# An attention and gated-MLP block on one core: first loads on two queues, and a new written-out order of all jobs

## The chip, the cores and the metric

The kernel runs on one core of a Trainium2 chip. The metric is the device time of one execution in microseconds. A core has TensorE (matmuls, written to PSUM), VectorE (DVE), ScalarE (ACT), GpSimd (POOL) and SyncE (SP), each with an instruction queue of its own that it works off in order; they wait for each other and for DMAs on semaphores.

## The reference

```python
x = A_x                                     # (1, 2048, 448), bfloat16
h = x + attention(layernorm(x))             # 16 heads of 28; token s sees s, s-2, ..., s-14
h2 = h + gmlp(layernorm(h))
# attention: qkv = x @ wqkv; logits = q . k * 28**-0.5 over the 8 offsets; softmax; @ v; @ wo
# gmlp: z = gelu(x @ w_in), w_in 448 x 1792; z1, z2 = the two halves of 896
#   g = w_sp (2048 x 2048) @ layernorm(z2) + b_sp[:, None];   return (z1 * g) @ w_out
```

Both layer norms are without scale and shift. All inputs are bfloat16.

## The kernel before

The 2048 tokens are 16 row tiles of 128 (`x_tm`), the 448 features three chunks of 128 and one of 64. The work is a list of 881 jobs, created in a fixed sequence by loops in the kernel's function and numbered as they are created. Each job belongs to one engine and is one or a few instructions with the resources that it reads and writes. `ORDER` is a list of job numbers, written out as a constant; `Planner.order` returns the jobs in that order, and each engine's queue gets its jobs in it. Semaphore waits follow from the resources alone, so any order that respects them computes the same. Job 880 is a filler: one matmul of 256 columns on a constant tile (`warm`), which keeps TensorE running; it stands in the list as often as wanted. `BANKS` gives each job group that needs PSUM its banks, in a list in the order of creation. `ON` names jobs that run on another engine than their default, `MODE` how the products are split.

The jobs, by their names (m a token tile, b one of 18 attention blocks of some 112 queries and 128 keys, t a group of token tiles, g a group of four heads):

- `x0`, `x1`, `x2`, `x4`, `x6`, `x8`, `x12` load 1, 1, 2, 2, 2, 4 and 4 tiles of x; `wq0` to `wq4` the query and key weights, `wv`, `wv_0`, `wv_1` the value weights, `wo...` the output weights, `w_in...` the MLP's, `bb` the bias b_sp, `w_out`; `wlo`, `whi` load w_sp through a DMA transpose. All DMAs stand on SyncE's queue before.
- `st0_m`, `mv0_m` (VectorE) and `rs0_m` (GpSimd) are the statistics of the first layer norm, `n0_m` (VectorE) normalizes into `xn`; `xT0` to `xT3` transpose on TensorE and `xe0_0`, `xe0_1`, `xe1_0`, `xe2_0`, `xe3_0` move the result to `xhT`; from `xT4` on the transpose is a DMA. `nd0_m`, `nd1_m`, `od_b` are small copies that a DMA transpose needs.
- `wp0` to `wp3` spread wq into padded heads (`wqk`). `qk0F0` to `qk0H` and `qk1...` are the first query-key products, `qk2_g` to `qk5_g` the wider ones, `qe...` their evacuations to `qkT`; `v_b` and `ve_b` the values for two blocks.
- `lg_b_j` (L791) are eight matmuls with 28 rows each, for eight heads' logits, j = 0 on the rows 0 to 63 and j = 1 on the rows 64 to 127; `ex_b_j` (ScalarE) the exponential, `mk_b` (VectorE) the mask, `o_b` (L815) 16 matmuls for the weighted values and the sums, `rc_b`, `om_b` (VectorE) the division into `otm`, `oT_b` a DMA transpose to `OT`, or from block 11 on to `OTs`, from where `oc_b` copies it to `OT`.
- `y_m` is the output projection for two tiles, `h_m` (VectorE) the first residual; `st1`, `mv1`, `rs1`, `n1` its layer norm, `hT_m` the DMA transpose to `hnT`.
- `z2_m` and `z1_u` are the MLP's products, `z2c` a raw evacuation, `z2g`, `z1g` the gelu (ScalarE); `st2`, `mv2`, `rs2`, `n2` the layer norm of z2. `g_i_n` (L964, L985) are the products with w_sp in pieces, `ua`, `um` (VectorE) bias and gate, `wo_m`, `wp12` to `wp15` (L1012, L1033) the last product, `r_m` the second residual, `out_m` the store.

A product of the 448 features (`product`, L459) has two jobs a and b that accumulate in one PSUM tile pair. The last chunk has 64 rows, and two matmuls on 64 rows each can stand in the two halves of the array. `MODE` 'FH' runs six full matmuls and then two half-row ones, 'HF' the other way round; 'AB' cuts the full ones into half-row ones too, 8 in job a and 6 in job b. So TensorE works with 128 rows, 64 rows or 28 rows, and changes between them along its queue.

TensorE's queue before, up to y12b (with x and a number: that many in a row):

```
before: warm x19 xT0 warm x8 qk0F0 qk0F1 qk0F2 qk0H xT1 warm x10 lg0_1 lg0_0 warm qk1F0 xT3 qk1F1 qk1F2 xT2 qk1H v0a
    qk2_3a v0b qk2_3b lg1_0 warm lg1_1 v2a qk2_0a qk2_2a v2b qk2_2b qk2_1a qk2_0b qk2_1b o1 v4a lg3_1 lg2_0 v4b lg2_1
    qk3_1a qk3_0a qk3_3a qk3_0b qk3_2a qk3_3b qk3_2b qk3_1b lg3_0 o0 o2 v6a lg5_1 lg5_0 v6b qk4_3a qk4_2a lg4_0 lg4_1
    qk4_3b qk4_2b qk4_0a lg6_1 qk4_0b qk4_1a lg6_0 o3 o5 lg7_1 qk4_1b y0a lg7_0 o4 lg8_0 o6 lg8_1 y0b v8a v10a lg9_0
    v10b v8b o7 qk5_3a qk5_2a lg9_1 lg11_0 qk5_2b qk5_3b y2a lg11_1 lg10_0 y2b qk5_0a lg10_1 qk5_0b y4a v12a qk5_1a
    y4b o8 qk5_1b lg12_0 v12b lg12_1 o9 lg13_1 o10 v14a lg13_0 v14b lg14_0 lg14_1 o11 o12 z2_1a lg15_1 z2_1b y6a
    lg16_1 lg15_0 y6b lg16_0 o14 o13 lg17_0 lg17_1 z2_0a z2_0b v16a z2_3a y8a v16b z2_2a y8b z2_2b o17 o16 z1_1a z2_4a
    z1_1b z2_3b z2_4b o15 z1_0a y10a z1_0b z2_5a y10b z2_5b z2_6a z1_5a z2_7a z2_6b z1_3a z2_7b y12a z1_3b y12b
```

Of the kernel before, what the change touches and what calls it, by code (L numbers as in the profile page):

```python
# [1111 lines left out]
```

## Time and profile before

| | us |
|---|---|
| median of 3 runs (lowest, highest) | 245.06 (244.08, 245.13) |
| profiled execution | 243.96 |
| its span, first to last instruction | 242.2 |
| TensorE busy | 236.7, 98% |
| VectorE, ScalarE, GpSimd busy | 149.7, 89.8, 37.7 |
| matmuls | 2568, 39 of them fillers |

In the views, PE is the matmul, PEld the weight load, SPq SyncE's queue. A line of the timeline is start, duration, engine, source line, operation, and the wait before it in brackets. A matmul's duration contains its way through the array, so that neighbours overlap; the chain that ended last shows them without overlap. The page's strips show 40 slices of 6.05 us in tenths of busy time. The windows' columns are stretch, its sum, busy time (and instructions) of PE, PEld, DVE, ACT and POOL, the granted clock, the DMA engines' share and GB/s.

### The profile page before, as it was taken

The numbers are of one execution on the slowest core, as the hardware profiler recorded it, in microseconds if no ns is written. First come the engines' busy times: TensorE is split into PE (matmuls) and PEld (weight loads), VectorE is DVE, ScalarE is ACT, GpSimd is POOL, SyncE is SP. The second block draws the span as 40 slices with busy tenths as digits, with TensorE's granted clock in tenths as the row PEclk, the third lists the DMA queues.
The fourth block names the chain that finished last, engine by engine and source line by source line (L and its number), as shares of the span: only waits on it lengthen the run. The fifth ranks groups of instructions, "written<-read, shape, count | busy, mean of one in ns | idle before, by whom it ended". The sixth has DMA issues, their size and how long they took to land.

```text
span 242.2 us, 5928 instructions
## 1 busy us (share of the span) xinstructions
PE 236.7 (98%) x2568; PEld 128.2 (53%) x2568; DVE 149.7 (62%) x336; ACT 89.8 (37%) x107; POOL 37.7 (16%) x90
## 2 busy tenths in 40 slices
PE   6999999999999999999999999999999999999995
PEld 4766545644655454555555555555555555555443
DVE  4799999989999999999800324320610663041834
ACT  4577467775998947959333000000000000000000
POOL 7432312120602023622300100000000000000000
DMA  5955755498477899945989700000100002010202
GB/s 167 293 152 103 117 107 121 138 145 186 97 119 152 165 182 197 194 90 120 164 179 170 152 3 0 0 3 0 41 0 3 1 3 76 0 41 0 78 0 76
DMA packets 66266, 23.21 MB, mean 96 GB/s; under 512 B 58688, under 2 KB 65984, under 8 KB 66240
## 3 DMA queue, kind: packets, MB, share of 16 engines
q1 hardware_dynamic: 66240, 22.83, 45.4%
q8 instruction: 20, 0.33, 0.6%
q14 instruction: 6, 0.05, 0.1%
HBM read 6.72 MB, written 1.84 MB: 35 GB/s over the span
## 4 chain that ended last, share of the span: by engine, by line
PE 80%; DMA 7%; ACT 5%; DVE 5%; SPq 2%; issue 0%; DVEq 0%
PE psum L964 37%; PE psum L459 26%; PE psum L1012 7%; ACT E L800 3%; PE psum L985 3%; DMA hnT<-xn 3%; PE psum L1033 2%; PE psum L791 2%; DMA x_tm<-in_A_x_dram 2%; PE psum L815 2%; DMA OTs<-otm 2%; SPq L517 2%; DVE st L875 1%; ACT V L502 1%; DVE z2p L502 1%; PE psum L692 1%
## 5 line engine op out<-in xcount | busy, mean ns | idle before, releaser
L945 DVE TENSOR_TENSOR ub<-psum,bb 128x512 bf16<-128x512 f32 x28 | 18.1, 685 | 43.1 <-PE psum L964 39.3
L964 PE MATMUL psum<-wsp_hi,z2p 64*128 64x512 bf16 x384 | 43.2, 376 | 0.0
L800 ACT ACTIVATE E<-psum 128x896 bf16<-128x896 f32 (+2 forms) x36 | 31.8, 935 | 8.1 <-PE psum L791 8.1
L964 PEld LDWEIGHTS psum<-wsp_hi,z2p 64*128 64x128 bf16 x384 | 21.7, 94 | 19.4
L875 DVE BATCH_NORM_STATS2 st<-z2p 128x6 f32<-128x448 bf16 x32 | 19.1, 614 | 12.8 <-ACT z2p L871 12.2
L964 PE MATMUL psum<-wsp_lb,z2p 64*128 64x512 bf16 x224 | 26.5, 376 | 0.0
L964 PE MATMUL psum<-wsp_la,z2p 64*128 64x512 bf16 x224 | 26.5, 376 | 0.0
L459 PE MATMUL psum<-w_in,hnT 64*128 64x448 bf16 (+1 forms) x200 | 25.4, 350 | 0.5 <-ACT E L800 0.3
L459 PE MATMUL psum<-hnT,w_in 64*128 64x512 bf16 (+1 forms) x178 | 24.7, 377 | 0.0
L993 DVE TENSOR_TENSOR srg<-psum,x_tm 128x448 bf16<-128x448 f32 (+1 forms) x17 | 9.5, 592 | 23.9 <-PE psum L1012 21.9
L459 PE MATMUL psum<-xhT,wqk 64*128 64x512 bf16 (+2 forms) x218 | 23.8, 349 | 0.2
L608 DVE BATCH_NORM_STATS2 st<-x_tm 128x6 f32<-128x448 bf16 x32 | 18.8, 612 | 2.3 <-DMA x_tm<-in_A_x_dram 2.2
L806 DVE TENSOR_TENSOR E<-E,maskb 128x1792 bf16<-128x1792 bf16 (+2 forms) x18 | 19.6, 1091 | 0.1
L913 ACT ACTIVATE z1p<-psum 128x1024 bf16<-128x1024 f32 x14 | 14.1, 1022 | 13.3 <-PE psum L459 13.1
L964 PEld LDWEIGHTS psum<-wsp_lb,z2p 64*128 64x128 bf16 x224 | 12.7, 94 | 11.4
L964 PEld LDWEIGHTS psum<-wsp_la,z2p 64*128 64x128 bf16 x224 | 12.7, 94 | 11.3
L603 POOL TENSOR_TENSOR rs<-rs,negh 128x2 f32<-128x2 f32 (+2 forms) x23 | 17.6, 764 | 1.9
L1012 PE MATMUL psum<-w_out,z1p 64*128 64x448 bf16 (+1 forms) x154 | 17.4, 349 | 0.0
L459 PEld LDWEIGHTS psum<-w_in,hnT 64*128 64x128 bf16 (+1 forms) x200 | 11.3, 94 | 11.5 <-issue 1.5
L459 PEld LDWEIGHTS psum<-xhT,wqk 64*128 64x128 bf16 (+1 forms) x218 | 10.5, 94 | 9.7 <-ACT E L800 0.5
L459 PEld LDWEIGHTS psum<-hnT,w_in 64*128 64x128 bf16 (+1 forms) x178 | 10.2, 94 | 9.9 <-ACT z2p L868 0.4
L459 PE MATMUL psum<-wv,xhT 64*128 64x448 bf16 (+1 forms) x114 | 14.6, 351 | 0.0
(64 smaller groups left out, 259.3 us busy)
## 6 DMA issues: line engine op xcount, KB each, us to landing
w_in<-in_B_w_in_dram SPq DMA_DIRECT2D x8, 224.0 KB, 3.4
out_dram<-srg SPq DMA_DIRECT2D x16, 112.0 KB, 1.7
x_tm<-in_A_x_dram SPq DMA_DIRECT2D x2, 448.0 KB, 5.8
w_out<-in_B_w_out_dram SPq DMA_DIRECT2D x1, 784.0 KB, 6.6
wq<-in_A_wqkv_dram SPq DMA_DIRECT2D x3, 224.0 KB, 2.8
x_tm<-in_A_x_dram SPq DMA_DIRECT2D x3, 224.0 KB, 4.8
bb<-in_B_b_sp_dram SPq DMA_DIRECT2D x1, 512.0 KB, 5.1
wv<-in_A_wqkv_dram SPq DMA_DIRECT2D x1, 336.0 KB, 5.3
```

The lines of the kernel that those rows point to most:

```text
L459: ins = e.matmul(o, w, x, start=k not in seen, stop=last, **kw)
L603: (lambda e: e.tensor_tensor(R, A, negh[:, 0:1].to_broadcast([128, n]), ALU.pow), [rr, r_negh], r_rs[k][m:m + n])],
L608: [(lambda e: e.bn_stats(st[:, m, :], src), [rsrc], [r_st[k][m]])], dve_t(D))
L800: return e.activation(o, i, AF.Exp, scale=SCALE)
L806: return e.tensor_tensor(a, a, maskb[:, 0:1, pad:pad + nq].to_broadcast([NK, NHEAD, nq]), ALU.mult)
L875: [(lambda e, m=m, k=k: e.bn_stats(st3[:, m, k, :], z2p[:, m, D * k:D * (k + 1)]), [r_z2[m]], [r_st[2][m]])], dve_t(D))
L913: return e.activation(o, i, AF.Gelu_apprx_tanh)
L945: [(lambda e: e.tensor_tensor(ub[:, s, :], psv(tk, k), bb[:, 512 * tc:512 * tc + 512], ALU.add), [r_bb], [r_ub[s]])], dve_t(512), use=[tk] ...
L964: ins = e.matmul(psv(tk, k), z2p[h, s, 128 * fc:128 * fc + 128], wsp(s, tc)[h], start=n == 0 and s == 0, stop=n == len(lots) - 1 and s == ...
L985: ins = e.matmul(psv(tk), z2p[:, s, 128 * fc:128 * fc + 128], wsp(s, tc), start=(s == 0), stop=(s == NB - 1))
L993: [(lambda e: e.tensor_tensor(srg[:, s, c0:c1], psv(tk, k, c1 - c0), x_tm[:, m, c0:c1], ALU.add), [r_x[m]], r_srg[2 * s + (c0 > 0):2 * s + ...
L1012: ins = e.matmul(psv(tk, k, D), z1p[h, fc, 128 * (m + k):128 * (m + k) + 128], w_out[h, fc, :], start=fc == 0 and (which == 0 or not half) ...
```

## The change

The changed kernel has the same jobs and instructions, but for two fillers more (41) and the modes of six products, four of which change the number of matmuls. New values stand for `ORDER`, `BANKS`, `MODE` and `ON`, and `load` lets `ON` choose the queue of a load. `half_t` and two durations have 2.5 ns more per matmul; they served the search and are not used when the order is written out. Of `MODE` six products change: `y8`, `z1_0`, `z1_4` to 'AB', `y10` to 'FH', `z2_0`, `z2_4` from 'HF' to 'FH'.

```diff
@@ load @@
             nload[0] += 1
-            return pl.job(name, eng, nload[0] * 0.001 - 65 if key is None else key,
-                          [(f, list(reads), list(writes), True)], dur, 0.0, after=after, srv=srv)
+            eng = ON.get(name, eng)
+            j = pl.job(name, eng, nload[0] * 0.001 - 65 if key is None else key,
+                       [(f, list(reads), list(writes), True)], dur, 0.0, after=after, srv=srv)
+            if not transpose and not name.startswith("out"):
+                j.alts = {"sp": dur, "act": dur + 0.08}
+            return j
@@ ON @@
+ON = {'x0': 'act', 'wq1': 'act', 'wq2': 'act', 'x1': 'act', 'wv': 'act', 'w_in1_1': 'act', 'w_in2_1': 'act',
+         'w_in3_0': 'act', 'xe1_0': 'dve', ..., 'wp0': 'act', 'wp3': 'act', 'qe3_0': 'dve', ..., 'bb': 'act'}
```

In `ON`, `qe1_1`, `qe2_2` and `qe3_1` are no longer on VectorE, so they fall back to ScalarE; `z2c6` and `z2c13` go to VectorE and `z2c9` back to ScalarE; `oc12` goes to ScalarE, `oc16` and `oc17` to VectorE; `wp0` changes places with `wp2`; and some of the small copies `nd` and `od` change between GpSimd and VectorE.

TensorE's queue after, up to y12b:

```
after: warm x21 xT0 warm x8 qk0F0 qk0F1 qk0F2 qk0H xT1 warm x11 lg0_0 lg0_1 qk1F0 qk1F1 qk1F2 qk1H warm xT3 xT2 v0a
    lg1_0 lg1_1 v0b qk2_3a qk2_0a qk2_3b qk2_0b v2a qk2_2a qk2_1a qk2_2b o1 qk2_1b v2b v4a lg2_0 lg2_1 v4b qk3_3a
    qk3_1a qk3_3b qk3_1b qk3_0a qk3_2a lg3_0 lg3_1 qk3_0b qk3_2b o0 o2 v6a lg4_1 lg4_0 v6b qk4_2a qk4_3a lg5_0 lg5_1
    qk4_2b qk4_3b qk4_0a lg6_0 qk4_0b lg6_1 qk4_1a o3 lg7_0 lg7_1 qk4_1b o4 y0a lg8_1 o6 o5 lg9_0 y0b v10a o7 lg8_0
    v8a v10b v8b qk5_2a qk5_0a lg9_1 lg10_0 qk5_2b qk5_0b y2a lg11_1 lg11_0 y2b qk5_3a lg10_1 qk5_3b y4a qk5_1a v12a
    y4b o8 v12b lg12_0 qk5_1b o9 lg12_1 v14a lg13_1 lg13_0 v14b o10 o11 lg15_0 lg14_1 z2_1a lg14_0 o12 lg16_1 z2_1b
    y6a lg15_1 lg16_0 y6b o14 o13 lg17_0 lg17_1 v16a z2_3a z2_0a z2_0b y8a v16b z2_3b y8b z2_2a z2_2b o17 o15 y10a
    z1_1a o16 z1_1b y10b z2_4a z2_4b z1_2a z2_5a z1_0a z2_5b y12a z1_0b y12b
```

The other queues at the start:

```
ScalarE before: tbl wp2 xe0_0 wp3 qe0_0 qe0_1 ex0_1 ex0_0 xe3_0 xe2_0
ScalarE after: x0 x1 wq1 wq2 tbl wv wp0 wp3 xe0_0 qe0_1 qe0_0 ex0_0 ex0_1 qe1_0 qe1_1 xe2_0 xe3_0
VectorE before: otmz wset st0_0 st0_1 mv0_0 mv0_1 wp0 n0_0 xe0_1 wp1 n0_1 st0_3 st0_2 mv0_3 mv0_2 st0_9 xe1_0 n0_3
    st0_5 st0_4 mv0_5 mv0_4 n0_2
VectorE after: wset otmz st0_0 mv0_0 st0_1 mv0_1 n0_0 wp1 xe0_1 n0_1 wp2 st0_3 st0_2 mv0_3 mv0_2 st0_8 xe1_0 st0_5
    st0_9 st0_4 mv0_9 mv0_5 mv0_4 n0_3 mv0_8 n0_2
SyncE before: x0 x1 wq0 wq2 wq3 wq1 wq4 x2 x8 wv_1 x4 wv x6 wv_0 wo_0 wo wo_1 x12 xT4 xT5 xT7 xT6
SyncE after: wq3 wq0 wq4 x2 x8 x4 x6 wv_1 wv_0 wo wo_0 x12 wo_1 xT5 xT4 xT6 xT7
```

And from the last attention blocks to the first gelus:

```
ScalarE before: ex12_0 ve12 ex12_1 ex13_1 ex13_0 ve14 ex14_0 ex14_1 ex15_1 z2c1 ex16_1 ex15_0 ex16_0 ex17_0 ex17_1
    oc11 z2g1 z2g0 ve16 oc14 z2c2 z2g2 z1g1 oc13 z2c4 z2g3 z2g4 z1g0
ScalarE after: w_in3_0 ve12 ex12_0 qe5_1 ex12_1 ex13_1 ex13_0 ve14 ex14_1 ex15_0 ex14_0 ex16_1 z2c1 ex15_1 ex16_0
    ex17_0 ex17_1 oc11 z2g1 z2g0 oc12 ve16 oc13 z2c2 z2g3 bb z2g2 oc14 z1g1 z2c4 z2g4 z1g0
SyncE before: oT10 wlo7 oT11 hT2 oT12 wlo12 hT4 oT14 oT13 wlo3 bb hT6 wlo4 wlo14 oT15 wlo15 wlo10 w_out hT8
SyncE after: oT10 hT2 hT4 oT11 wlo13 oT12 oT13 wlo12 oT14 wlo7 wlo10 oT15 wlo4 hT6 oT16 wlo15 w_out oT17 hT8
```

From there on the same products, gates and output rows stand in another order; and from `g10_1b` on TensorE's queue is the same.

More of the change, by code (lines that the diff above doesn't have):

```diff
@@ L80 @@
 WINB = 2
-ON = {'xe1_0': 'dve', 'nd0_5': 'dve', 'nd0_6': 'dve', 'nd0_7': 'dve', 'nd0_8': 'dve', 'nd0_12': 'dve', 'nd0_13':
-         'dve', 'nd0_15': 'dve', 'wp2': 'act', 'wp3': 'act', 'qe1_1': 'dve', 'qe2_2': 'dve', 'qe3_0': 'dve', 'qe3_1':
-         'dve', 'qe4_0': 'dve', 'qe4_3': 'dve', 'qe5_2': 'dve', 'od1': 'dve', 'od2': 'dve', 'nd1_0': 'dve', 'nd1_1':
-         'dve', 've4': 'dve', 'nd1_3': 'dve', 'od5': 'dve', 've6': 'dve', 'nd1_7': 'dve', 'od9': 'dve', 'oc11': 'act',
-         'nd1_8': 'dve', 'od12': 'dve', 'oc13': 'act', 'nd1_10': 'dve', 'nd1_11': 'dve', 'oc14': 'act', 'oc16': 'act',
-         'od17': 'dve', 'oc17': 'act', 'nd1_15': 'dve', 'z2c3': 'dve', 'z2c5': 'dve', 'z2c9': 'dve'}
+ON = {'x0': 'act', 'wq1': 'act', 'wq2': 'act', 'x1': 'act', 'wv': 'act', 'w_in1_1': 'act', 'w_in2_1': 'act',
+         'w_in3_0': 'act', 'xe1_0': 'dve', 'nd0_4': 'dve', 'nd0_5': 'dve', 'nd0_6': 'dve', 'nd0_7': 'dve', 'nd0_8':
+         'dve', 'nd0_13': 'dve', 'nd0_14': 'dve', 'nd0_15': 'dve', 'wp0': 'act', 'wp3': 'act', 'qe3_0': 'dve',
[3 rows of a table added]
+         'dve', 'z2c3': 'dve', 'z2c5': 'dve', 'z2c6': 'dve', 'z2c13': 'dve', 'bb': 'act'}
 RAW2 = [0, 1, 2, 1, 1, 1, 1, 2, 1, 2, 1, 0, 0, 1, 0, 0]
@@ L442, in half_t @@
         def half_t(c):
-            return max(c / 2400.0, c / 4800.0 + 0.045)
+            return max(c / 2400.0 + 0.0025, c / 4800.0 + 0.045)
         def act_t(c):
@@ L970, in gate_pair @@
                 j = pl.job("g%d_%d%s" % (i, n, ab), "pe", GK + 2 * i + 0.01 * n + (2.5 if n and not fine else 0), [(f, rws, [])],
-                           512 / 2400.0 * len(ss), acq=tk if n == 0 else None, use=[tk], kind="H",
+                           (512 / 2400.0 + 0.0025) * len(ss), acq=tk if n == 0 else None, use=[tk], kind="H",
                            after=[prev] + (z2_jobs if i >= 3 and n == 0 else []))
@@ L1018, in out_pair @@
             for j in (j1, j2):
-                j.modes = [("FF", full_t(D, FC7), "F"), ("FF", full_t(D, FC7), "F"), ("AB", FC7 * D / 2400.0, "H")]
+                j.modes = [("FF", full_t(D, FC7), "F"), ("FF", full_t(D, FC7), "F"), ("AB", FC7 * half_t(D), "H")]
             j1.mate, j2.mate = j2, j1
```

4 lines of the change are left out of this document (2 added, 2 removed), and 93 rows, old and new, of tables (BANKS, MODE, ON, ORDER).

## The prediction

> **What bounds the kernel now.** I read the page first: the busy time of each engine, the slices, the chain that ended last.
>
> ```profile
> span 242.2 us, 5928 instructions
> PE 236.7 (98%) x2568; PEld 128.2 (53%) x2568; DVE 149.7 (62%) x336; ACT 89.8 (37%) x107; POOL 37.7 (16%) x90
> PE   6999999999999999999999999999999999999995
> DVE  4799999989999999999800324320610663041834
> ACT  4577467775998947959333000000000000000000
> 234.28 5.33 PE psum L1033 x35
> ```
>
> TensorE is busy in all but 5.5 us of the span. The chain's last stretch of matmuls ends at 234.28 + 5.33 = 239.6, so 2.6 us of the idle time is the tail behind the last matmul, which the change does not touch. VectorE is at nine tenths or more in nearly every slice from 12 to 97 us, ScalarE only here and there. Next, the waits of TensorE:
>
> ```profile
> PE psum L1054 <- DVE warm L577: 1.9, 1, 1.9
> PE psum L459 <- ACT E L800: 0.3, 1, 0.3
> PE psum L459 <- DMA hnT<-xn: 0.2, 1, 0.2
> ```
>
> 1.9 us is the wait for the memset of the fillers' operand; all others, with one of 0.15 that the start below shows, are 0.7. So the order keeps TensorE fed although VectorE is full. A new order can lower the time only in three ways: the first useful matmuls start sooner, the same products occupy TensorE for less time, or the remaining waits go. The columns that the matmuls stream do not change: an "AB" product runs 14 half-row matmuls, an "FH" or "HF" one 6 full and 2 half-row. The rows of the output projection have both forms:
>
> ```profile
> L1012 PE MATMUL psum<-w_out,z1p 64*128 64x448 bf16 x140 | 14.7, 349 | 0.0
> L1012 PE MATMUL psum<-w_out,z1p 128*128 128x448 bf16 x14 | 2.8, 353 | 0.0
> ```
>
> A half-row matmul costs 0.105 us (14.7/140), a full one 0.20 (2.8/14): the same array time, so the changed modes cost nothing by themselves.
>
> **The start.** TensorE's timeline up to the job qk1F0, from which it has useful work all the time:
>
> ```profile
> 1.92 4.19 PE L1054 MATMUL psum<-warm 128*128 128x256 bf16 x19 [1.92 <-DVE warm L577]
> 5.94 0.33 PE L649 MATMUL psum<-ident,xn 128*128 128x128 bf16 x3
> 6.38 1.05 PE L1054 MATMUL psum<-warm 128*128 128x256 bf16 x8
> 7.27 1.83 PE L692 MATMUL psum<-xhT,wqk 128*128 128x128 bf16 x32
> 9.48 1.27 PE L1054 MATMUL psum<-warm 128*128 128x256 bf16 x10
> 10.68 0.42 PE L791 MATMUL psum<-qkT 28*128 28x128 bf16 x16
> 11.47 0.62 PE L692 MATMUL psum<-xhT,wqk 128*128 128x128 bf16 x8 [0.15 <-DVE xhT L502]
> ```
>
> The first 19 fillers take (5.94 - 1.92)/19 = 0.212 us each, the next eight (7.27 - 6.38)/8 = 0.111: the array runs at half speed until about 5.9, 4.0 us after its first matmul. After the change VectorE clears the fillers' operand first, not behind otm's memset (0.48 us, below), so the fillers start at about 1.44. There are 21 of them: at 0.212 each they end at 5.89; if the speed doubles 4.0 us after the first again, at about 5.7. xT0 then starts at 5.7 to 5.9, against 5.94. What follows up to lg0 has the same instructions but 11 fillers for 10: 10.68 - 5.94 + 0.11 = 4.85, so lg0 starts at 10.55 to 10.75. The pair lg0 takes 0.33 with the switch behind it (rows below), and the filler that stood behind lg0 is gone: qk1F0 at 10.9 to 11.1, for 11.47 now. I take 0.5 us. That holds only if its operands are there:
>
> ```profile
> 0.97 0.48 DVE L583 MEMSET otm<- 128x512 uint32 x1 [0.97 <-PEq L1097]
> 5.30 0.40 DVE L619 TENSOR_SCALAR xn<-x_tm,mv,rs 128x448 bf16<-128x448 bf16 x1 [0.47 <-POOL rs L603]
> 10.19 0.63 DVE L608 BATCH_NORM_STATS2 st<-x_tm 128x6 f32<-128x448 bf16 x1 [0.62 <-DMA x_tm<-in_A_x_dram]
> 10.74 0.67 DVE L502 CAST xhT<-psum 128x512 bf16<-128x512 f32 x1
> 0.79 1.28 ACT L594 ACT_TABLE_LOAD   x1 [0.79 <-PEq L1097]
> 4.98 0.95 ACT L502 ACTIVATE wqk<-wq 128x896 bf16<-128x896 bf16 x1 [2.33 <-DMA wq<-in_A_wqkv_dram]
> 0.79 0.88 SPq L517 DMA_DIRECT2D x_tm<-in_A_x_dram  x2
> 1.71 2.64 SPq L517 DMA_DIRECT2D wq<-in_A_wqkv_dram  x5
> 5.02 5.15 DMA x_tm<-in_A_x_dram
> 2.00:8.00 6.00, 6.00 (x46) 4.53 (x47) 3.30 (x9) 2.18 (x5) 4.46 (x15) 1.00 0.86 236
> 8.00:14.00 6.00, 5.85 (x96) 4.46 (x95) 5.18 (x15) 3.62 (x6) 1.78 (x4) 1.00 1.09 315
> ```
>
> n0_0 (5.30) waits for GpSimd; with mv0_0 moved ahead of st0_1 it comes some half a us sooner, and is not last. What held qk1F0 is the chain issue, DMA, st0_9, xe1_0: VectorE stood before a statistic of x8, issued ninth on SyncE at 5.02 and landed 5.15 later, with the evacuation xe1_0 (10.74) behind it. In the new order a statistic of x8 (st0_8) still stands ahead of xe1_0, but x8 is SyncE's fifth issue: at 0.44 to 0.53 us per issue (0.88/2, 2.64/5) about 3.0, two us sooner. Ahead of it are x0, x1, five wq and x2 with 1.26 MB (by their shapes), with x8 itself 1.72 MB; from 2.0 us at the windows' 236 to 315 GB/s it lands between 7.5 and 9.3. VectorE needs some 1.2 us from there to the end of xe1_0 (two rows, start to start 0.55 and 0.6): 8.7 to 10.5, so the fillers decide, not the load.
>
> Here a rule of the Trainium skill speaks against the change: the page "DMA: Bandwidth & Descriptors", section "Issuing engines are not separate DMA queues", says that transfers from several issuing engines share the same 16 DMA engines and interleave, so that a second issuer saves only issue time, usually small. By it x8 would land when the bytes allow; the trace agrees that the engines are nearly full (share 0.86, then 1.09), but not before 8 us, and the sum uses only the bytes.
>
> ScalarE now issues x0, x1, wq1, wq2 before its table load and wv behind it. No row shows an issue on ScalarE; SyncE's 0.44 to 0.53 bound it from below, and twice that I take as the upper end. At SyncE's price four take 1.9: the table load ends near 4.0, wv and the two casts of wq (0.95, and some 0.6 for the half-width one) end near 6.3, and xe0_0 is done by about 6.8, ahead of qk0F0 at 7.0 to 7.2. At twice the price everything is 2.4 later and TensorE waits 2 us at qk0F0, of which the shorter rest hides nothing.
>
> **What TensorE spends.** The chain's pieces give the price of a logits job (L791, eight matmuls) and of a change between full rows, half rows (64) and quarter rows (28):
>
> ```profile
> 20.86 0.50 PE psum L815 x16
> 22.21 0.33 PE psum L791 x16
> 23.22 0.30 PE psum L791 x8
> 30.17 0.90 PE psum L815 x32
> ```
>
> A single lg costs 0.30 with the switch behind it, but two neighbours of different halves (j = 0 and 1 use different rows) cost 0.33 together: the second runs beside the first. Two o jobs cost 0.90, one 0.50: a switch is 0.10. Read off the two orders of TensorE from qk1F0 on: of the 34 lg jobs 8 pairs and 18 singles stand before, 12 pairs and 10 singles after. That is 18 x 0.30 + 8 x 0.33 = 8.04 against 10 x 0.30 + 12 x 0.33 = 6.96: 1.08 us less, four switches included. All switches from there fall from 73 to 67; the two not yet counted are 0.2. Together 1.27 us. Since TensorE has no slack, this comes off one to one unless another engine cannot follow.
>
> **The waits.** Besides the rows above, waits hide where a job lasts longer than its like:
>
> ```profile
> 70.61 0.40 PE L791 MATMUL psum<-qkT 28*128 28x114 bf16 x16
> 71.28 1.04 PE L459 MATMUL psum<-w_in,hnT 64*128 64x448 bf16 x5 [0.28 <-ACT E L800]
> ```
>
> From 70.61 to 71.28 a pair takes 0.67 for 0.33, at a place where exponentials follow each other on ScalarE. With the 0.2 for hnT that is half a us; I take about a us for all, an estimate. Which go and which come? In the new order sixteen evacuations again follow each other on ScalarE between v12 and ex17_1, so I keep half a us there; z2_8, which waited for hnT, stands near where it did, while n1_8 and n1_9 have less ahead of them in VectorE's queue, so that wait should go. VectorE loses three evacuations (qe1_1, qe2_2, qe3_1) to ScalarE; ScalarE's slices from 12 to 30 (7, 7, 4) hold these 2 us. One more evacuation of z2, net, goes to VectorE behind 85 us, and small copies change places. Three w_in loads move to ScalarE, at 0.44 to 0.53 each, where its slices are 7, 7, 5, and are hidden there; bb (one issue) falls behind z2g3 where they are 8 and 9, with z2g2 behind it: 0.5 us of delay there if the cover is gone. On SyncE nine issues go, and the transposes move up. I put new waits against old ones at nothing, between 0.7 gained and 1 lost.
>
> Sum: 0.5 + 1.27 + 0 = 1.8 us off the span of 242.2, 240.4. The profiled execution took 243.96, so 242.2 after; it lies 1.1 below the median of the runs shown, 245.06, from which the same 1.8 give 243.3. A measurement of this kernel can tell about 0.5%, 1.2 us, from no change.
>
> **The rivals.** First, the start is not gained. ScalarE's wv (0.34 MB) interleaves with x8: 2.06 MB at 236 GB/s land at 10.7, xe1_0 ends at 11.9 and qk1F0 starts at 12.0, half a us later than now. Or ScalarE's issues are dearer than SyncE's, up to the 2 us at qk0F0. Against 1.27 saved later stand 0 to 1.5 lost here: 243.8 to 245.3, and 244.3 with wv's half us. For it speaks that xe0_0 and qk0F0 have less than half a us between them; against it that wv is issued late, behind the table load. The rule on shared DMA engines would act in this way.
>
> Second, TensorE's saving is eaten where ScalarE sets the pace, 57 to 85 us: the pairs ask for two exponentials at once, and each later one waits. Then only the start and the switches stay, less half a us for bb: 244.4. The wait of the last fence speaks for it, ScalarE's 63% idle against it.
>
> Third, slower. y10a is a product of the attention output:
>
> ```profile
> 72.14 0.61 DVE L826 TENSOR_TENSOR otm<-psum,rcp 114x448 bf16<-114x448 f32 x1
> 78.93 1.47 PE L459 MATMUL psum<-hnT,w_in 128*128 128x512 bf16 x6
> 83.96 0.93 PE L459 MATMUL psum<-wo,OT 64*128 64x448 bf16 x8
> 77.22 4.05 DMA OTs<-otm
> DMA to landing us min/median/max: 2.5/3.0/6.1
> ```
>
> It stood at 83.96. From z1_1's start, 78.93, to there are 5.0 us, of which the rest of z2_3 and o15 (0.7) stay ahead; o16 (0.4, half of a row of two o) goes behind: so y10a moves up by 4.7, and by some 1.6 of the savings, to 77.6. It needs oc11 to oc13, and oc13 needs the transposed otm of block 13. Before, that transfer started at 77.22 and took 4.05. Now it must start by 77.6 - 0.6 (the copy) - 4.05 = 72.9, and otm of block 13 (written at 72.14 to 72.8 before) exists no earlier than about 71.5. If it queues behind two transposes of some 1.3 us on SyncE and lands after the longest 6.1, oc13 ends at 71.7 + 2.6 + 6.1 + 0.6 = 81.0 and TensorE waits 3.4 us: 245.06 - 1.8 + 3.4 = 246.7. It decides from 1.8 us of wait on. For it: landings of 6.1 us do occur; against it: SyncE has nine issues fewer, the median is 3.0, and a us of slack is left.
>
> **How the numbers follow.** Forecast 0.58, its own range 242.4 to 243.9; the start not gained 0.17; ScalarE's pace 0.13; slower 0.12. Most of the forecast and a third of the first rival lie more than 1.2 us below 245.06: faster 0.59. Same 0.28, slower 0.13. The range runs from 241.8 (waits gone, start 0.7 better) to 245.3, which leaves out the third rival and little else.
>
> **What would show it.** In the changed profile, right: qk1F0 (L692) at 10.9 to 11.1; L791 pieces of 16 in twelve places; TensorE without a wait over 0.5 us; y10a near 77.6 to 78. Wrong: x8's landing past 10 or qk0F0 past 7.4 (first rival), VectorE or ScalarE without idle time and TensorE waiting for E in many places (second), a wait of TensorE for ScalarE's copy from OTs or for hnT of more than 1.8 us (third).

## The result and the profile after

The changed kernel is slower: median 245.80 us in 20 runs (244.35 to 250.68), against 244.57 in 20 runs of the kernel before (243.87 to 245.34) on the same chips. The ratio is 1.0049 with a 95% interval of 1.0027 to 1.0070, that is 1.2 us, no more than the prediction said could be told from no change. The forecast of 243.3 us was wrong in sign, and 245.80 lies above its range, which ended at 245.3. The base of its sum, 245.06 from three runs, was itself 0.5 above the median of 20. The ratios here and below leave out runs of over 1.5% more than the fastest of their kernel, so that some medians below lie further up than their ratios.

The profiled execution after took 244.35 us with a span of 242.6; it is the fastest of its 20 runs. So the profile shows the change at its best, 0.4 us behind the profiled run of before (243.96), and hides most of what the median lost. Its page has these lines in place of those quoted of before (busy time by engine; busy tenths in 40 slices; the last stretch of TensorE in the chain):

```profile
span 242.6 us, 5957 instructions
PE 235.9 (97%) x2582; PEld 119.5 (49%) x2582; DVE 148.8 (61%) x334; ACT 89.7 (37%) x108; POOL 39.1 (16%) x91
PE   7899999999998999999999999999999999999995
DVE  4899799979978999999823009330303173141834
234.66 5.33 PE psum L1038 x35
```

TensorE is busy 0.8 us less (235.9 for 236.7), in the direction of the forecast, yet its last matmul ends at 239.99 instead of 239.61. The two new digits 8 in its strip are the slices from 6 to 12 and from 73 to 79 us. The waits of TensorE name the places:

```profile
PE psum L1059 <- DVE warm L582: 1.4, 1, 1.4
PE psum L697 <- ACT xhT L503: 1.1, 1, 1.1
PE psum L460 <- ACT z2p L876: 0.9, 1, 0.9
PE psum L460 <- ACT V L503: 0.5, 1, 0.5
```

The first is shorter by 0.5, as forecast. The other three are new. TensorE's timeline at the start, and where the last two fall (start, duration, what, wait before it in brackets):

```profile
5.66 0.33 PE L654 MATMUL psum<-ident,xn 128*128 128x128 bf16 x3
8.25 1.83 PE L697 MATMUL psum<-xhT,wqk 128*128 128x128 bf16 x32 [1.10 <-ACT xhT L503]
12.13 1.84 PE L697 MATMUL psum<-xhT,wqk 128*128 128x128 bf16 x32
60.72 0.37 PE L796 MATMUL psum<-qkT 28*128 28x114 bf16 x8
65.02 0.93 PE L460 MATMUL psum<-w_in,hnT 64*128 64x448 bf16 x8 [0.53 <-ACT V L503]
77.49 1.60 PE L460 MATMUL psum<-w_in,hnT 64*128 64x448 bf16 x8 [0.94 <-ACT z2p L876]
79.74 1.31 PE L460 MATMUL psum<-wo,OT 128*128 128x448 bf16 x6
```

In order: xT0, qk0F0, qk1F0, lg12_1, z2_1a, z2_2a, y10a. The same lg12_1 stood here before:

```profile
60.76 0.37 PE L791 MATMUL psum<-qkT 28*128 28x114 bf16 x8
61.06 0.56 PE L815 MATMUL psum<-V,E 128*128 128x29 bf16 x16
```

Between these marks the 0.4 us can be split. The start: qk1F0 at 12.13 for 11.47, 0.66 lost where 0.5 was forecast as gained. The middle, from qk1F0 to lg12_1: 48.59 (60.72 - 12.13) for 49.29 (60.76 - 11.47), 0.70 gained. The rear, from lg12_1 to the end of the last matmul: 179.27 (239.99 - 60.72) for 178.85 (239.61 - 60.76), 0.42 lost. That makes 0.38.

The mark at lg12_1 does not cut the same work in both orders. The second row of before is o9, which stands behind lg12_1 there; the new order runs it ahead:

```profile
60.24 0.56 PE L820 MATMUL psum<-V,E 128*128 128x29 bf16 x16
```

From its start to the next job's are 0.48 us here (60.72 - 60.24) and 0.50 there (61.56 - 61.06). For the same work the middle is thus about 1.2 shorter, and the rear loses about 0.9. At the pair lg17_0, lg17_1 both orders have done the same products:

```profile
70.32 0.72 PE L796 MATMUL psum<-qkT 28*128 28x114 bf16 x16
```

From qk1F0 to there the new order takes 58.19 (70.32 - 12.13), the old 59.14 (70.61 - 11.47, by its row in the prediction): 0.95 gained. Behind it 0.67 is lost (169.67 for 169.00).

The windows of before and after, up to 61 us and from there to 97, agree (stretch, its sum, then busy time and instructions of PE, PEld, DVE, ACT, POOL, the clock, the DMA share, GB/s):

```profile
12.00:61.00 49.00, 48.84 (x725) 26.29 (x722) 47.02 (x103) 33.81 (x42) 12.02 (x22) 1.00 0.65 136
61.00:97.00 36.00, 35.54 (x456) 18.42 (x452) 34.47 (x82) 30.15 (x36) 9.15 (x23) 1.00 0.78 149
```
```profile
12.00:61.00 49.00, 49.00 (x761) 26.46 (x749) 44.94 (x100) 37.38 (x46) 12.29 (x23) 1.00 0.59 118
61.00:97.00 36.00, 34.53 (x446) 18.03 (x444) 33.49 (x81) 28.01 (x34) 10.75 (x25) 1.00 0.90 176
```

From 12 to 61 us TensorE is never idle (0.16 before); from 61 to 97 it is idle 1.47 us (36.00 - 34.53) where it was 0.46. The DMA engines carry less than before in the first stretch and more in the second.

### The profile page after: what moved, and what is told of

Same layout as the page of the kernel before. It is cut to its first block, busy times and chain, and to the rows that moved or that the text cites. A ratio compares the mean times of both kernels' runs of the same rounds, so it can differ in the third digit from the quotient of the medians.

```text
span 242.6 us, 5957 instructions
## 1 busy us (share of the span) xinstructions
PE 235.9 (97%) x2582; PEld 119.5 (49%) x2582; DVE 148.8 (61%) x334; ACT 89.7 (37%) x108; POOL 39.1 (16%) x91
## 4 chain that ended last, share of the span: by engine, by line
PE 80%; DVE 9%; DMA 6%; ACT 2%; POOL 1%; issue 1%; SPq 0%
PE psum L969 37%; PE psum L460 24%; PE psum L1017 7%; PE psum L990 3%; PE psum L796 3%; DMA OTs<-otm 3%; PE psum L1038 2%; PE psum L820 2%; DMA wq<-in_A_wqkv_dram 2%; DVE st L880 2%; DMA hnT<-xn 2%; PE psum L697 1%; DVE st L613 1%; DVE x_tm L763 1%; DVE E L811 1%; DVE xn L624 1%
## 5 line engine op out<-in xcount | busy, mean ns | idle before, releaser
L969 PEld LDWEIGHTS psum<-wsp_hi,z2p 64*128 64x128 bf16 x384 | 18.7, 94 | 22.5 <-DVE ub L950 0.2
L460 PEld LDWEIGHTS psum<-w_in,hnT 64*128 64x128 bf16 (+1 forms) x200 | 11.1, 94 | 13.2 <-ACT z2p L876 1.4
L969 PEld LDWEIGHTS psum<-wsp_la,z2p 64*128 64x128 bf16 x224 | 11.2, 94 | 12.9
L969 PEld LDWEIGHTS psum<-wsp_lb,z2p 64*128 64x128 bf16 x224 | 10.9, 94 | 13.2 <-DVE z2p L889 0.2
L607 POOL TENSOR_SCALAR rs<-mv 128x2 f32<-128x2 f32 (+2 forms) x23 | 5.5, 238 | 55.9 <-DVE mv L615 38.7
```

What stands on the lines that cost most here:

```text
L460: ins = e.matmul(o, w, x, start=k not in seen, stop=last, **kw)
L969: ins = e.matmul(psv(tk, k), z2p[h, s, 128 * fc:128 * fc + 128], wsp(s, tc)[h], start=n == 0 and s == 0, stop=n == len(lots) - 1 and s == ...
```

## The experiments

The question was where 1.2 us in the median, and some 3 us against the forecast, had gone. The theory: the rear of the new order, behind 61 us, puts products right behind the transposes and loads that feed them, so that TensorE waits wherever a transfer lands late. The rivals: the start alone; the loads that went to ScalarE's queue (bb, w_in), whose bytes slow the transposes on SyncE's; one late load, w_in3_1; and the mere luck of executions. The diffs show a queue's entries, with a neighbour or two.

**The start's casts.** e1 lets ScalarE evacuate xT0 (`xe0_0`) ahead of the two casts of wq; e2 does the same and puts all first loads back on SyncE.

```diff
 ScalarE:  wv
-wp0 wp3 xe0_0
+xe0_0 wp0 wp3
```

> The changed kernel with one thing moved: on ScalarE xe0_0 stands ahead of wp0 and wp3. Theory A (the start is lost because ScalarE, in order, casts wp0 and wp3, 6.42 to 7.74, before it evacuates xT0, which was ready at 6.1): xe0_0 runs at 6.1, wp0 ends at about 7.1, qk0F0 starts at 7.1 to 7.2 instead of 8.25, xT1 and the fillers follow, lg0 stands at 10.7, and qk1F0 starts when xe1_0 is done, 11.2 to 11.3 instead of 12.13: 0.8 us less than the changed kernel in the profile and in the median, so about 245.0 beside 244.6 for the kernel before. Rival B (the loads' bytes set the start, whatever the order on ScalarE): qk1F0 stays at 12.1 and the time at 245.8. On the spread of the changed kernel (244.4 to 250.7 in 20 runs, before 243.9 to 245.3) A says nothing.

e1: 245.68 us, ratio 1.0025 [1.0002, 1.0047]. qk0F0 starts at 7.80 (a wait of 0.43 stays behind it, put down to VectorE) and qk1F0 at 11.68: 0.45 of the 0.66 came back. The wait at 65 stays (0.4), the one at z2_2a is 1.1, and a new one of 0.9 stands at lg10_0. So the start is a part of the loss in this profile, and not all. The ratio alone, with its interval, doesn't tell e1 from the changed kernel.

```diff
 e1, and:
-ScalarE: x0 x1 wq1 wq2 tbl wv     SyncE: wq3 wq0 wq4 x2 x8 ...
+ScalarE: tbl                      SyncE: x0 x1 wq0 wq2 wq3 wq1 wq4 x2 x8 wv_1 x4 wv ...
```

> As the run with xe0_0 ahead, and all first loads back on SyncE in the order of the kernel before (only w_in1_1, w_in2_1, w_in3_0 and bb stay on ScalarE). Theory A: wq0 lands at about 4.4 instead of 6.4 as in the kernel before, wp0 ends before xe0_0, qk0F0 starts at 7.1 behind the fillers, as with two queues and xe0_0 ahead; x8 lands at 10.2, st0_8 and xe1_0 follow, qk1F0 at 11.4 to 11.5. So the split queues bring nothing at the start, and the time is within 0.3 us of the run with xe0_0 ahead: 245.0 to 245.3. Rival B: the split itself costs, and one queue gains 0.7 or more on the changed kernel beyond what xe0_0 gains. The spread: if it comes from two queues' loads sharing the DMA engines, the runs fall back into 1.5 us as with the kernel before; if it comes from a later place (oT11's transpose, on whose landing ScalarE waits), it stays at 3 us and more.

e2: 247.23 us, 1.0065 [1.0029, 1.0101]; the runs still spread from 244.61 to 249.65. wq0 landed at 4.40, as before (4.41), against 6.40 after, but on ScalarE wp0 now stood behind xe0_0, and qk0F0 started at 8.01: this run was badly laid out for the start. It shows two things all the same. With one queue, and with wq0 ahead of wq3 on it, the first weights land 2 us sooner; and the spread does not come from the two queues at the start.

**Repairs of the rear.** z2_2a's wait after the change goes back to ScalarE, which stands 1.3 us before the copy oc11:

```profile
73.79 0.58 ACT L503 ACTIVATE OT<-OTs 128x456 bf16<-128x456 bf16 x1 [1.30 <-DMA OTs<-otm]
```

e3 therefore moves hT4 behind oT11 on SyncE; e4 joins that with e1 and with x8's statistic behind xe1_0; e5 brings w_in3_1 ahead of hT0; e6 joins all of these and moves oc14, wq0 and some of TensorE's products.

```diff
e3  SyncE:   -hT2 hT4 oT11 wlo13          +hT2 oT11 hT4 wlo13
e4  e3, e1, and VectorE:  -st0_8 xe1_0    +xe1_0 st0_8
e5  SyncE:   -hT0 wlo2 w_in3_1 oT8        +w_in3_1 hT0 wlo2 oT8
e6  e4, e5, and SyncE:  -wq3 wq0          +wq0 wq3
    ScalarE: -z2g2 oc14 z1g1 z2c4         +z2g2 z1g1 z2c4 oc14
    TensorE: z1_0b z1_2b ahead of y12a, z1_5a ahead of y12b, z2_7a ahead of z1_3a
```

> The changed kernel with one thing moved: on SyncE hT4 stands behind oT11 instead of ahead of it. Theory C (the wait of 0.9 us at z2_2a comes from SyncE: oT11 is ready at 67.1, but hT2 and hT4 take SyncE until 71.2, so oc11, the gelu's table load, z2g1 and z2g0 on ScalarE are 1.2 us late, and z2_2a waits for z2g0's bank): oT11 is issued at about 68.9, oc11 starts right behind ex17_1 at 72.5, the wait at z2_2a goes, 0.9 to 1.1 us less than the changed kernel: 244.8 in the median. And as all that follows hangs on the landing of oT11, the spread shrinks if it came from there. Rival D (ScalarE is at its limit there by its own work, exponentials and table load): oc11 moves, but z2_2a or another product waits about as long, gain under 0.3 us. Price if hT2 is the late one: none, it keeps its place.

e3: 246.84, 1.0046 [1.0019, 1.0073]. The wait at z2_2a is gone. In its place z2_1a waits 1.2 for w_in3_1, and z1_2a 1.6 for a gelu behind oc14, whose transfer oT14 landed 6.15 after its issue (2.51 after the change).

> Both moves together, and on VectorE st0_8 behind xe1_0. If A and C hold and add up: qk1F0 at 10.9 to 11.1 (the statistic of x8 no longer stands ahead of xe1_0), no wait at z2_2a, so 1.1 + 1.0 = 2.1 us less than the changed kernel: 243.7 in the median, 0.9 below the kernel before, which is what TensorE's saving of 1.2 us should give. If B and D hold: 245.5 or more.

e4: 247.06, 1.0035 [1.0004, 1.0066]. qk1F0 starts at 11.44, level with the kernel before (11.47), and yet the time stayed. z2_1a waits 1.3 at 65.41, y12a 1.1 for the copy of oT15 (5.39 to landing). Behind the first wait the windows show the granted clock (the column behind POOL) at half speed:

```profile
64.00:65.00 1.00, 0.11 (x6) 0.00 (x0) 1.00 (x2) 1.00 (x2) 0.49 (x1) 1.00 0.84 87
67.00:68.00 1.00, 1.00 (x18) 0.57 (x17) 0.80 (x3) 0.92 (x2) 0.00 (x0) 0.50 0.87 176
69.00:70.00 1.00, 1.00 (x8) 0.30 (x4) 0.13 (x1) 0.84 (x1) 0.23 (x1) 0.50 2.52 179
```

From 67 to 70 it is 0.50, in the microsecond before 0.95 and in the one behind 0.85: some 3.2 us at half speed, about 1.6 us of work, an estimate from these rows. In this execution a wait cost more than its own length. The mean granted clock of each run shows how often that happens: it lies at 0.985 to 0.993 in 10 of e4's 12 runs and in 6 of the changed kernel's 20, and at 0.999 or more in all 146 runs of the kernel before that stand beside the experiments.

> The changed kernel with one load moved: on SyncE w_in3_1 stands ahead of hT0 and wlo2 (issue near 57) instead of behind them (60.7 to 61.2). Theory E: z2_1a needs this load; in the changed kernel it landed 64.8 in its own profile but 65.2 to 65.5 in the four runs of the first round, when z2_1a (started 65.0, 65.4 to 66.1) could have gone on from about 64.3; before it landed at 62.8, 2.8 us ahead of z2_1a. When TensorE has stood there for over a us, the granted clock can fall to 0.5 for 3 us (0.74 between 64 and 70 us in the run with both moves), which costs 1.6 us more. By E the load lands near 61, z2_1a waits only for ve14 (0.5 us as in the changed kernel's profile), the granted clock stays at 1.00 from 64 to 70, the median falls by 0.5 to 1 us (to 245.0 or so) and the runs over 247.5 become rare. Rival F (the spread comes from the attention transposes oT11 to oT15, whose landings took 2.4 to 6.2 us): median and spread as in the changed kernel, 245.8 and 6 us.

e5: 246.01, 1.0034 [1.0001, 1.0067]. w_in3_1 lands at 62.2 instead of 64.8, and z2_1a still waits 0.44, now for the values' evacuation ve14. oT15 took 5.99 and y12a waited 1.3; lg10_0 1.0, z2_2a 0.8.

> The changed kernel with slack put back at all places where a run waited: xe0_0 ahead of wp0 and wp3, wq0 ahead of wq3, st0_8 behind xe1_0, w_in3_1 ahead of hT0, hT4 behind oT11, oc14 behind z2c4 on ScalarE, y12a and y12b two products later. If the lost time is waits for late landings and the order of ScalarE at the start, TensorE's 1.2 us of saving and 0.3 to 0.5 of start come through: qk1F0 near 11.2, waits between 60 and 92 us below 0.6 together, granted clock 1.00, median 243.5 to 244.0, 0.8 below the kernel before, spread 2 us. If the new order as such needs more from VectorE and ScalarE than they give (their rows between 64 and 78: 12 of 14 us busy), the waits turn up elsewhere, 245 or more.

e6: 249.99, 1.0173 [1.0127, 1.0219], the worst of all. The chain, and then SyncE, ScalarE and TensorE in its timeline, show why:

```profile
79.67 8.23 DMA OTs<-otm
```
```profile
79.67 1.20 SPq L517 DMA_TRANSPOSE OTs<-otm  x1
80.12 0.37 ACTq L518 DMA_DIRECT2D bb<-in_B_b_sp_dram  x1
90.30 0.93 PE L460 MATMUL psum<-w_in,hnT 64*128 64x448 bf16 x8 [3.55 <-DVE otm L831]
```

oT14 is issued at 79.67, and bb's 512 KB follow from ScalarE 0.45 later. oT14 lands after 8.23 us, VectorE stands behind it, and TensorE waits 3.55. After the change bb came 1.75 behind oT14 (issues at 77.97 and 79.72), which landed after 2.51. These repairs, each chosen from the trace of an earlier run, made together a kernel that is 1.7% slower.

**One late load or bb in the old order.** e7 delays w_in3_1 in the kernel before, behind wlo7; e11 issues bb there from ScalarE.

```diff
e7   SyncE:   -wlo2 w_in3_1 oT8 ... oT10 wlo7    +wlo2 wlo7 w_in3_1 oT8 ... oT10
e11  SyncE:   -wlo3 bb hT6                       +wlo3 hT6
     ScalarE: -z2g0 ve16                         +z2g0 bb ve16
```

> The kernel before with the suspected cost put in: on SyncE wlo7 stands ahead of w_in3_1 instead of behind oT10, so that w_in3_1 is issued near 60.5 to 61.5 instead of 59.1 and lands at 64.5 to 66 instead of 62.8, with z2_1a at 65.6. Theory E: z2_1a now waits for the landing in part of the runs, by 0 to 1.5 us, some of them with a granted clock below 1, and the tight 1.5 us of the kernel before widen to 3 us or more with a median 0.3 to 1 us higher. Rival F: no change, 244.6 and 1.5 us of spread.

e7: 245.48, 1.0006 [0.9986, 1.0026]. w_in3_1 lands at 66.0, later than after the change, and z2_1a waits 0.42, but the time is that of before. One late load is not the cause by itself.

> The kernel before with one load moved to ScalarE: bb is issued behind z2g0, near 76.4, half a us behind oT14's issue (75.9) and ahead of oT13's (77.2), instead of on SyncE at 80.6. Theory H: oT14 and oT13 land 4 to 8 us after their issues instead of 2.5 and 2.5 to 4, oc14 on ScalarE (78.5 before) comes 2 to 4 us later, z2c2 behind it too, z2_4a waits for that bank: 1 to 4 us slower, 246 to 248.5, with a wider spread. If only the order of the jobs matters and not which queue issues a load: 244.6 to 245.1 as before.

e11: 245.75, 1.0020 [0.9986, 1.0054], 243.82 to 248.45: no difference that the interval shows, though a wider spread. oT14 took 3.87 instead of 2.53 to land, and TensorE did not wait for it. But bb did not go out where it was meant to, half a us behind oT14:

```profile
73.05 0.39 ACTq L517 DMA_DIRECT2D bb<-in_B_b_sp_dram  x1
73.47 1.28 ACT L868 ACT_TABLE_LOAD   x1
75.62 0.90 ACT L871 ACTIVATE z2p<-psum 128x896 bf16<-128x896 f32 x1
```

It stands behind z2g0 (75.62) in ScalarE's queue and was issued before it, 2.15 ahead of oT14 (75.20). So e11 shows what an early bb does in the old order. It leaves open what one close behind a transpose would do there.

**The late loads back on SyncE in the new order.** e8 returns bb, e9 all four, e10 adds the repairs of e4 and e5 (w_in3_1 behind hT0).

```diff
e8   ScalarE: -z2g3 bb z2g2      +z2g3 z2g2
     SyncE:   -oT15 wlo4         +oT15 bb wlo4
e9   e8, and w_in1_1, w_in2_1, w_in3_0 from ScalarE to SyncE
     (behind w_in0_1, behind oT7, ahead of hT0)
```

> The changed kernel with bb (512 KB) back on SyncE, behind oT15. Theory H, from the traces so far: a load issued by ScalarE runs beside the transposes that SyncE has in flight, and these then land late. bb was issued 1.7 us behind oT14 or less, and oT14 landed 2.4 to 2.6 us after its issue when bb just missed it, 4.2 and 4.3 twice, 6.2 with bb 0.7 us behind it and 8.2 with bb 0.4 behind it; oT15, which follows, took 3.8 to 6.0 in every run of the new order and 2.6 in both runs of the old one. oc14 and oc15 wait for them, and z1_2a (3.1 to 4.6 lost in two runs) or y12a (1.3 in two runs) wait for those. By H oT14 and oT15 now land 2.4 to 2.7 us after their issues, z1_2a and y12a do not wait, the median falls by about 0.7 us to 245.1 and the spread narrows to 3 us. Rival F' (those transposes are late by their own queue, w_sp's transposes ahead of them): oT15 still takes 4 us or more, no gain.

> The changed kernel with all four late loads back on SyncE: bb behind oT15, w_in1_1 behind w_in0_1, w_in2_1 behind oT7, w_in3_0 ahead of hT0. By H also oT4, oT5 (4.1 to 6.5 us beside w_in2_1 from ScalarE in the changed kernel and two of its variants, 2.9 before) land in 3 us, om7 does not wait for otm and lg10_0 not for om7 (1.1 us lost in two of six profiles). What stays of the known losses: the start (0.7), z2_1a (0.5 to 1.3, w_in3_1), z2_2a (0.9). Median 244.6 to 245.0, spread 2 to 2.5 us. If ScalarE's late loads are innocent: 245.8 and 5 us.

> The kernel with the late loads on SyncE, and xe0_0 ahead of wp0 and wp3, st0_8 behind xe1_0, hT4 behind oT11, w_in3_1 ahead of wlo2. If the causes found are all: qk1F0 at 11.2 to 11.5 (before 11.47), z2_1a and z2_2a wait 0.5 together, TensorE's occupancy is 1.2 below that of the kernel before, so the median is 243.4 to 244.0, 0.6 to 1.2 under it, spread 2 us. If the order as such is too tight: 245 or more, with waits at new places.

e8: 246.25, 1.0049 [1.0011, 1.0087]; e9: 245.93, 1.0055 [1.0018, 1.0093]; e10: 247.31, 1.0048 [1.0008, 1.0088]. The transfers did what was hoped: oT15 lands after 3.24 and 3.31 (e8, e9) instead of 4.12, in e9 oT4 after 3.41 instead of 4.12. But hT6 now queues behind bb on SyncE, and e9's timeline has the price, 1.56 us (1.30 in e8, 3.24 in e10):

```profile
90.94 2.34 PE L460 MATMUL psum<-hnT,w_in 64*128 64x512 bf16 x20 [1.56 <-DMA hnT<-xn]
```

So the queue that the loads stand on is not the cause by itself either. The waits move and the time stays.

**The order cut in two.** The remaining runs join the orders. h1 runs the new one up to lg12_1 and the old one from there; h2 the old one up to v12b and then the new; h3 the old start up to qk1F0, the new middle to lg12_1, the old rear; h4 is like h3 with the joint at lg17_1. Part of h2's output differs from the reference's, for a reason at its joint that was not found; its time is read for the order alone.

```diff
h1  new ... lg12_1 | old          h2  old ... v12b | new
h3  old ... qk1F0 | new ... lg12_1 | old
h4  old ... qk1F0 | new ... lg17_1 | old
```

> New order (with its queues, banks and modes) up to TensorE's job lg12_1, near 60.7, and from there all remaining jobs in the old order. 12 of the new order's 13 neighbouring lg pairs lie in the new part. Theory S (the loss lies behind 61 us, where the new order has each product stand close behind the transposes it needs): the start costs 0.1 to 0.7 as in the profiles of the changed kernel, the stretch to lg12_1 is 0.6 to 0.7 shorter than in the old order (48.6 against 49.3), behind it all as before: 244.3 to 245.0 in the median, spread 2 to 3 us, no run with a lowered granted clock. Rival T (the loss is spread over the whole new order, first loads and w_in loads beside transposes): 245.5 or more with a spread over 4 us.

> Old order up to v12b (near 60), then the remaining jobs in the new order, bb on ScalarE among them. Theory S: start at 11.47 as before, but from 61 to 95 us the waits of the changed kernel (z2_1a, z2_2a, z1_2a or y12a, z1_5a), 2 to 4 us together against 1, runs with a lowered clock, 246 to 247 in the median, spread over 4 us. Rival T: 244.8 or less, spread as before.

> Old order up to qk1F0 with all first loads on SyncE, new order from there to lg12_1 but with w_in1_1, w_in2_1 and w_in3_0 on SyncE, then the old order. Theory S: start 11.5, the stretch to lg12_1 0.6 to 0.7 shorter, the rest as before: 243.9 to 244.2 in the median, 0.6 below the kernel before, spread 2 us. Rival T: no gain, 244.8 or more.

> As the last, with the second joint at lg17_1 (near 70.7) instead of lg12_1, so that z2_1a, y6, lg13 to lg17 and hT2, hT4, oT11 on SyncE stand as in the new order. If the stretch from 61 to 71 us is one of the lossy ones (z2_1a waiting for w_in3_1 or ve14, 0.5 to 1.3 us; oc11 late behind hT4, 1 us): 0.5 to 1.5 us slower than the joint at lg12_1, with a wider spread. If only what follows 71 us loses: equal to it within 0.3.

h1: 244.42, 0.9982 [0.9959, 1.0005]; h2: 246.24, 1.0058 [1.0037, 1.0079]; h3: 244.83, 1.0000 [0.9979, 1.0021]; h4: 246.77, 1.0077 [1.0051, 1.0103]. With the new start and middle, the old rear is better than the new by 0.0067 (1.0049 - 0.9982), 1.6 us; behind the old start and middle the new rear costs 0.0058, 1.4 us. This is the verdict that the repairs could not give: the new start and middle together are even or slightly better (0.9982), and the loss lies behind 61 us. With its order the new rear brings its own engines, banks and the six changed modes of products, all of which stand there; the joints do not tell these apart. h3 should have been the best of the four, but its joint at qk1F0 makes v4a wait 0.4 at 22 us, and it reaches lg12_1 at 61.34, 0.7 later than h1 (60.63), although it started qk1F0 0.55 sooner. h4 has four waits behind its joint (0.7, 0.3, 0.9 and 0.8), so it doesn't show whether the stretch from 61 to 71 is at fault by itself.

**The version to keep.** h5 is h1 with the start laid out for the landings as they are: wp0 on VectorE, all casts in the order in which their weights land, xe0_0 ahead of ScalarE's one cast, x8's statistic behind xe1_0, w_in3_1 ahead of wlo2. h6 also issues three w_in from SyncE. e12 has h5's start and w_in3_1 and then the new order to its end.

```diff
 ScalarE: wv
-wp0 wp3 xe0_0
+xe0_0 wp3
 VectorE: n0_0
-wp1 xe0_1 n0_1 wp2 st0_3 st0_2 mv0_3 mv0_2 st0_8 xe1_0
+wp0 xe0_1 wp1 wp2 n0_1 st0_3 st0_2 mv0_3 mv0_2 xe1_0 st0_8
```

> The kernel joined new to old at lg12_1, with the start put in the order that the landings ask for: wp0 back on VectorE behind n0_0, then xe0_1, wp1, wp2, n0_1; on ScalarE xe0_0 ahead of wp3; st0_8 behind xe1_0; and w_in3_1 ahead of wlo2 on SyncE. The loads stay on two queues, so wq0 lands at 5.8 to 6.4. If the order of the casts was what lost the start: wp0 done at 6.8, qk0F0 at 7.2 to 7.4 (8.15 in the joined kernel's profile), xe1_0 at 10.1 to 10.8, qk1F0 at 11.0 to 11.2 (12.03), 0.8 us off: 243.4 to 243.8 in the median, 1 us under the kernel before. If the loads' shared landing decides alone: qk1F0 at 11.6 or later, 244.2 to 244.6.

> As the last, with w_in1_1, w_in2_1 and w_in3_0 back on SyncE. If these loads beside oT4 and oT5 cost in part of the runs (om7 late, lg10_0 waiting 1.1 us), the spread is smaller and the median up to 0.3 us lower than with them on ScalarE; if not, the two agree within 0.3 us.

> The changed kernel with the start of the fastest joined one (wp0 on VectorE, xe0_0 ahead of wp3, st0_8 behind xe1_0, w_in3_1 ahead of wlo2), and the new order to the end. Theory S (the loss lies behind 61 us): qk1F0 at 10.8 to 11.2 and lg12_1 near 59.5 to 60.7 as in the joined kernels, then waits at z2_1a, z2_2a, z1_2a, y12a or z1_5a: 1.5 to 2.5 us slower than the joined kernel, 244.8 to 245.8 in the median, spread over 3 us. Rival (the loss was the start and w_in3_1): 243.4 to 244.2 as the joined kernel.

h5: 243.36 us, 0.9922 [0.9898, 0.9946], faster than both kernels (242.97 to 244.62 in six runs). h6: 244.16, 0.9964 [0.9941, 0.9987]. e12: 244.86, 1.0001 [0.9973, 1.0030]. h5's timelines of TensorE and VectorE:

```profile
6.96 1.84 PE L697 MATMUL psum<-xhT,wqk 128*128 128x128 bf16 x32
10.85 1.84 PE L697 MATMUL psum<-xhT,wqk 128*128 128x128 bf16 x32
6.17 0.39 DVE L503 COPY wqk<-wq 128x896 bf16<-128x896 bf16 x1 [1.02 <-DMA wq<-in_A_wqkv_dram]
```

qk0F0 at 6.96 and qk1F0 at 10.85 are the forecast's 7.0 to 7.2 and 10.9 to 11.1, although wq0 landed no sooner than 6.15: the fault was the order of the casts, not the bytes. h5 differs from h1 by this start and w_in3_1, and is 0.0060 lower, 1.5 us; e12 differs from the changed kernel by the same, and is 0.0048 lower, 1.2 us. e12 differs from h5 in the rear alone: 0.0079 more, 1.9 us. Against h6 it is 0.9 us, which the intervals hardly tell from none. Since the profiled run of h5 is its slowest and that of e12 its fastest, the two traces look alike from 61 to 97 us (34.91 and 34.93 busy); the medians differ. In h5 oT4 took 6.30 to land beside w_in2_1, issued from ScalarE 0.16 after it, and lg10_0 waited 0.73 behind; in h6, with w_in2_1 on SyncE, oT4 took 4.22 and nothing waited there:

```profile
PE psum L460 <- DMA hnT<-xn: 0.5, 1, 0.5
PE psum L796 <- ACT qkT L503: 0.4, 1, 0.4
PE psum L460 <- ACT E L805: 0.3, 1, 0.3
```

These are all of h6's waits beside the fillers', and its profiled run took 242.89, the lowest seen. In the medians h6 isn't better than h5, so that this wait is worth its 0.7 us is not shown.

## Why the prediction was wrong

**The array's time was right.** 1.27 us was forecast for pairs and switches. For the same work, o9 counted, the middle came out 1.2 shorter, of it 0.16 an idle time that went; and in the rear, with 1.01 more of idle time from 61 to 97 us, 0.9 was lost at the end. So TensorE spent 1.0 less in the middle and some 0.1 less behind it, 1.1 in all. That fits the place of the pairs: of the four that the new order has more, three stand ahead of lg12_1.

**The start failed at "xe0_0 is done by about 6.8".** The fillers (1.38, xT0 at 5.66) came as forecast, ScalarE's price per issue too: its queue shows 0.87 for two, 0.94 for two and 0.54, SyncE's price. What was left out is the landing of the weights. ScalarE's timeline, and a row of the chain:

```profile
1.70 0.94 ACTq L518 DMA_DIRECT2D wq<-in_A_wqkv_dram  x2
2.67 1.28 ACT L599 ACT_TABLE_LOAD   x1 [2.67 <-issue]
2.73 0.54 ACTq L518 DMA_DIRECT2D wv<-in_A_wqkv_dram  x1
6.42 1.42 ACT L503 ACTIVATE wqk<-wq 128x896 bf16<-128x896 bf16 x2 [2.26 <-DMA wq<-in_A_wqkv_dram]
7.74 0.36 ACT L503 ACTIVATE xhT<-psum 128x256 bf16<-128x256 f32 x1
```
```profile
1.42 4.97 DMA wq<-in_A_wqkv_dram
```

The casts were taken to end near 6.3, as if their operand were there; wq0, issued 0.3 earlier than before, landed 2.0 later (6.40 for 4.41), with x0, x1, wq1 and wq2 on their way beside it from the other queue. In e6, where wq0 is SyncE's first issue, it landed at 3.91, and x0 and x1 at 4.13 and 4.34 instead of 3.04 and 3.44: there wq0 came first, and x0 and x1 came later. xe0_0 stood behind both casts and ended at 8.10. The first rival had the time (qk1F0 at 12.0, measured 12.13) by the wrong chain: it put the delay on x8, which landed at 9.96, late as the rival said and past the 7.5 to 9.3 of the sum, but xe1_0 began at 10.57, was done at 11.3 and did not decide. The rule of the Trainium skill quoted in the prediction (page "DMA: Bandwidth & Descriptors", section "Issuing engines are not separate DMA queues") was borne out and given too little weight: x8 was issued 1.8 us sooner and landed 0.2 sooner. It was applied to x8 alone and should have been applied to the first transfer that anything waits for. With the casts in the order of the landings the same two queues gave the forecast's start (h5), worth 1.2 to 1.5 us in the runs (with w_in3_1 moved too).

**The waits, "at nothing, between 0.7 gained and 1 lost", were the other error.** By the joined kernels the new rear costs 1.4 to 1.9 us, at least as much as the start. The term compared two orders by the landings of one profiled execution, as if they were fixed. By the traces they are not: oT15 landed between 3.81 and 5.99 us after its issue in the new rears with bb on ScalarE, 2.53 to 3.04 in the old; oT14 between 2.4 and 8.2. In the old order the readers stood further behind. w_in3_1 landed at 62.81 there, 2.8 us ahead of its first use, z2_1a:

```profile
65.64 0.93 PE L459 MATMUL psum<-w_in,hnT 64*128 64x448 bf16 x8
```

In the new order it landed at 64.78, 0.24 ahead of z2_1a at 65.02. A search that is given durations as traced can use up exactly this slack. That TensorE's idle time from 61 to 97 rose from 0.46 to 1.47 in the best of 20 runs is shown; that the further us in the median is such waits too, at other places in other executions, is what the other kernels' traces suggest (1.7 to 2.8 us idle there in e1 to e5), but no profile of a slower execution of the changed kernel itself was had. The lowered clock is a small part of it: the median of the 14 runs without it is 245.50, 0.3 below the median of all.

**bb was priced as an issue.** "0.5 us of delay" on ScalarE was right for the issue (0.37 in its row) and left out its 512 KB beside the transposes. In the kernel as changed that is small (oT15 4.12 for some 3.3); how much of the 1.2 us it makes is open, since returning it (e8) moved the wait to hT6, and e11 did not bring it close behind a transpose.

**The other rivals.** The third rival's wait did not occur: oc13 ended at 79.19 and y10a started at 79.74 without one. Its kind, a product moved up to its transposed operand, is what struck elsewhere. ScalarE's pace (the second) is not seen: no wait for E in the waits above.

What stays open: which place behind 61 us costs how much. Single repairs (e3, e5, e8, e9) only moved the waits, the rear's order was not tried apart from its engines and modes, and h4's joint spoils the one run that would have split the stretch.

## What to carry to other kernels

An order searched with traced durations can be tuned to one execution: compare, for each transfer, the time from landing to first use before and after, and treat slack below the spread of the landings (here 2.4 to 6 us) as a wait to come. When loads move to a second queue, work out anew when the first needed one lands, and order the work behind it by that. If repairs only move the waits, cut the two orders at a place where both have done the same work, and keep the better part of each.
